# Sparse attention with a bilinear feed-forward layer: the second chunk's products no longer kept in DRAM, and the queries of a chunk loaded in two transfers

## The chip, the cores and the metric

The kernel runs on one core of a Trainium2 chip. The metric is the device time of one execution in microseconds; lower is better. Engines are written as in the profile: PE is TensorE, DVE VectorE, ACT ScalarE, POOL GpSimd, SP the engine whose queue issues transfers.

## What is computed

Four sequences of 768 tokens with 8 heads of 64 pass block-sparse attention; its output, laid out as a matrix x of 3072 x 512, passes a bilinear layer with 1536 inner features.

```python
def _attn_ref(q, k, v, sampled_blocks):             # q, k, v: (4, 8, 768, 64)
    scores = scale * np.matmul(q, k.transpose(0, 1, 3, 2))
    # blocks of 32: neighbours, the first and last block, 3 sampled blocks per row of blocks
    ...
    scores = np.where(mask, scores, -1000000000.0)
    attn = np.exp(scores - np.max(scores, axis=-1, keepdims=True))
    attn = attn / (np.sum(attn, axis=-1, keepdims=True) + 1e-09)
    return np.matmul(attn, v)

def _moe_ref(x, w_a, w_b, w_out):                   # x: (3072, 512)
    a = x @ w_a                                     # w_a, w_b: (512, 1536)
    b = x @ w_b
    return a * b @ w_out                            # w_out: (1536, 512)

x = attn_out.transpose(0, 2, 1, 3).reshape(B * S, H * D)
```

## The kernel before

**Chunks and units.** The 3072 tokens are cut into 12 chunks of 256, three for each sequence, and a chunk into 8 units of 32 tokens (one block). The chunks come in the order 1, 0, 2 for the first sequence and 0, 1, 2 for the others; "second chunk" means the second in this order, `cc == 1`. A unit in the middle of a sequence attends 8 blocks: POOL copies their keys into `KG`, SP's queue gathers their values into `VG`. The first and the last unit of a sequence attend all 768 tokens, in quads of heads (`attend_quad`).

**Attention of a unit.** PE makes the scores `s` (lines 772 and 873), DVE their maxima (`low`, line 888 or 975), ACT the exponentials `sm` (898 or 990), ACT or DVE a high and DVE a low half-precision part `hl` (790, 793, 797); a transposing transfer on SP's queue turns `hl` into `pt` (920, 1015), and PE multiplies `pt` with the values (`av`, 816). ACT and DVE write x as a high and a low part into `xT` (1060, 1063), which has two buffers, one for each parity of the chunk. `x_ready[cc]` fires when all of a chunk's x is written.

**Queries.** `queries(cc)` loads 64 x 2048 numbers of f32 (64 partitions, head by head, 256 tokens each) in one transfer from ACT's queue (634), takes a bound of them (642), scales them into the high part of `QT` (647), makes the low part (649) and has both copied to partitions 64 to 127 by two transfers on SP's queue (673).

**Feed-forward of a chunk.** It goes in 12 slices f of 128 features. `first_products` makes both products of a slice in `ab` (24 matmuls, line 1098; two buffers). `inner` has ACT scale the first into `a` (1126) and DVE multiply it by the second (1129). `split` makes `gh`, a rounded copy, on ACT (1153) and the rest `gl` on DVE (1156), two buffers each. `second_products` multiplies them by the slice of `w_out` into `o` (6 matmuls, lines 1184 to 1186). `store` copies `o` (1199, 1200) and writes the rows out (1203). The weights are loaded and split into parts during the first chunks (lines 693 to 753); `w_ready[f]` fires per slice.

**Parking.** With `PARK`, the second chunk's products take another way: `inner` stores `a` to a DRAM tensor `parked_g` (1134) in place of the split, and `unpark`, started when `second_products` comes to that chunk, loads each slice back into a buffer of `a` (1147; the tile is named `u`) and splits it there. The first products of the second chunk are a flow of their own, ranked one behind that of all other chunks, and the third chunk's first products wait for the last split of the second (`split_done`).

**The order of the work.** The instructions' order is set when the kernel is built, by a planner (`Plan`). Each piece of work is a generator (a flow) with a rank; it asks for a `Way`: an engine, a cost in ns, a function that issues the instructions, and for transfers the time that the DMA engines are taken to move. The planner keeps its own clock of each engine and of the DMA engines and issues at each step the request that can begin first; at equal times the lower rank goes first. Attention's ranks are its unit numbers, those of `second_products` 8000, of `first_products` 9000. So a changed cost or a removed flow changes the order of other work, too. Within an engine the instructions run in the order in which they were issued.

## Time and profile before

| | |
|---|---|
| median of 3 runs | 906.45 us (903.02 to 914.17) |
| profiled execution | 901.24 us |
| its span, first to last instruction | 899.5 us |
| mean granted TensorE clock | 0.977 |
| busy: PE, weight loads, DVE, ACT, POOL | 770.2, 619.3, 580.0, 464.3, 176.9 us |
| transfers | 145.50 MB, 212221 packets |

The profile is of one execution. Times are counted from the first instruction. "Busy" is the time in which an engine had at least one instruction running; issuing transfers is not counted. A wait is the idle time of an engine before an instruction, put down to what ended last of all that the instruction needed. The chain is followed back from the last instruction, at each step to what released it or to the instruction before it on its engine. A granted clock of 1 is TensorE's full speed.

### The profile page before, as it was taken

What the parts mean: (1) busy time and instruction counts of PE and PEld (TensorE: products, weight loads), DVE (VectorE), ACT (ScalarE), POOL (GpSimd) and SP (SyncE); (2) the same over time, 40 slices, a digit from 0 to 9 for tenths busy, and PEclk for the clock granted to TensorE, in tenths of its full rate; (3) what the DMA queues carried; (4) which work ended last, traced back from release to release, by engine and by line L of the source; (5) the groups of instructions that cost most, each with busy time, mean ns of one, the idle gap of its engine ahead of it and who ended that gap; (6) DMA issues with size and microseconds to landing.
All of it is one profiled execution on the core that took longest, in us unless ns stands there. A gap on an engine that the chain in (4) does not pass through costs nothing.

```text
span 899.5 us, 23840 instructions
## 1 busy us (share of the span) xinstructions
PE 770.2 (86%) x9024; PEld 619.3 (69%) x9024; DVE 580.0 (64%) x1533; ACT 464.3 (52%) x1118; POOL 176.9 (20%) x416
## 2 busy tenths in 40 slices
PE   0132499678989999999999899999998999999998
PEld 0022277557768777777777678788776878888886
DVE  3898999986558677665677577645867736342222
ACT  4675576586446566754456468335536424232222
POOL 0652142322003332110132331001322200000000
PEclk9998599899999999999999999999999999999999
DMA  9978999979878699985867999637766516351000
GB/s 228 287 186 218 243 235 252 222 193 206 215 205 181 140 194 210 198 181 136 173 155 170 180 211 206 153 82 159 180 134 155 125 29 153 80 121 27 25 1 24
DMA packets 212221, 145.50 MB, mean 162 GB/s; under 512 B 152841, under 2 KB 180490, under 8 KB 211338
## 3 DMA queue, kind: packets, MB, share of 16 engines
q1 hardware_dynamic: 201280, 106.22, 54.3%
q10 hardware_dynamic: 10826, 37.76, 14.4%
q8 instruction: 71, 1.16, 0.5%
q14 instruction: 44, 0.36, 0.1%
HBM read 87.82 MB, written 14.16 MB: 113 GB/s over the span
## 4 chain that ended last, share of the span: by engine, by line
PE 55%; DMA 14%; DVE 10%; ACT 7%; issue 2%; SPq 2%; ACTq 0%; POOL 0%
PE ab L1098 30%; PE o L1184 6%; PE av L816 5%; DMA pt<-hl 5%; PE o L1186 5%; PE o L1185 5%; DMA q<-in_q_dram 3%; PE s L772 3%; DVE low L888 1%; DVE hl L797 1%; DVE xT L1063 1%; DMA VG<-vd 1%; DVE QT L649 1%; DMA u<-parked_g 1%; ACT sm L898 1%
## 5 line engine op out<-in xcount | busy, mean ns | idle before, releaser
L1098 PE MATMUL ab<-xT,wab 128*128 128x256 f16 x3456 | 404.7, 274 | 12.7 <-ACT xT L1060 6.9
L1098 PEld LDWEIGHTS <-wab 128*128 128x128 f16 x3456 | 329.7, 98 | 78.5 <-issue 37.7
L1129 DVE SCALAR_TENSOR_TENSOR a<-a,rscale,ab 128x256 f32<-128x256 f32 x144 | 68.6, 478 | 112.1 <-ACT a L1126 110.9
L1184 PE MATMUL o<-woh,gh 128*128 128x512 f32 x288 | 127.1, 441 | 6.8 <-ACT gh L1153 6.4
L1126 ACT ACTIVATE a<-ab,f 128x256 f32<-128x256 f32 x144 | 67.5, 468 | 120.3 <-PE ab L1098 114.4
L898 ACT ACTIVATE sm<-s,low,cq 128x256 f32<-128x256 f32 x176 | 97.9, 559 | 58.7 <-DVE low L891 29.4
L816 PE MATMUL av<-pt,VG 128*128 128x64 f16 x2688 | 103.2, 196 | 28.9 <-DMA pt<-hl 14.9
L816 PEld LDWEIGHTS <-VG 128*128 128x128 f16 x2688 | 94.6, 100 | 48.1 <-issue 35.5
L573 POOL COPY KG<-keysT 128x384 int32<-128x384 int32 x88 | 56.9, 647 | 356.5 <-PE s L772 325.9
L797 DVE SCALAR_TENSOR_TENSOR hl<-sm,den,hl 128x256 f16<-128x256 f32 (+1 forms) x208 | 104.3, 510 | 21.4 <-ACT hl L790 18.6
L1186 PE MATMUL o<-woh,gl 128*128 128x512 f32 x288 | 115.2, 400 | 0.5 <-DVE gl L1156 0.5
L1185 PE MATMUL o<-wol,gh 128*128 128x512 f32 x288 | 113.6, 395 | 0.0
L578 POOL COPY KG<-keysT 128x128 int32 x264 | 94.5, 394 | 42.9 <-POOL KG L573 23.2
L1153 ACT CAST gh<-a 128x256 fp32r<-128x256 f32 x132 | 53.1, 403 | 59.2 <-DVE a L1129 58.0
L1156 DVE TENSOR_TENSOR gl<-a,gh 128x256 fp32r<-128x256 f32 x132 | 58.2, 441 | 32.3 <-ACT gh L1153 31.6
L1184 PEld LDWEIGHTS o<-woh,gh 128*128 128x128 f32 x288 | 54.7, 190 | 27.7 <-ACT gh L1153 10.0
L772 PE MATMUL s<-KG,QT 128*32 128x256 f16 x1408 | 58.8, 291 | 16.8 <-DMA QT<-QT 16.6
L873 PE MATMUL s<-mrows,ident 128*32 128x192 bf16 (+1 forms) x352 | 25.6, 280 | 54.7 <-ACT sm L898 27.8
L1063 DVE SCALAR_TENSOR_TENSOR xT<-av,xT 64x256 f16<-64x256 f32 x96 | 40.4, 421 | 44.3 <-ACT xT L1060 43.4
L1186 PEld LDWEIGHTS o<-woh,gl 128*128 128x128 f32 x288 | 54.6, 189 | 16.6 <-DVE gl L1156 4.3
L888 DVE TENSOR_REDUCE low<-s 128x2 f32<-128x512 f32 x88 | 59.9, 682 | 6.4 <-PE s L772 6.1
L772 PEld LDWEIGHTS <-QT 128*32 128x32 f16 x1664 | 43.7, 101 | 29.5 <-issue 24.1
(92 smaller groups left out, 736.0 us busy)
## 6 DMA issues: line engine op xcount, KB each, us to landing
VG<-vd SPq DMA_DIRECT2D x284, 64.0 KB, 2.2
VG<-vd SPq DMA_DIRECT2D x88, 192.0 KB, 3.3
VG<-vd SPq DMA_DIRECT2D x32, 384.0 KB, 3.8
q<-in_q_dram ACTq DMA_DIRECT2D x12, 512.0 KB, 6.0
QT<-QT SPq DMA_DIRECT2D x24, 256.0 KB, 3.8
vd<-vs SPq DMA_DIRECT2D x16, 384.0 KB, 4.1
out_dram<-ou SPq DMA_DIRECT2D x24, 256.0 KB, 2.4
stage<-in_k_dram ACTq DMA_DIRECT2D x12, 384.0 KB, 4.2
```

Of the source, the lines that this page charges most:

```text
L578: nc.gpsimd.tensor_copy(to[:, :, (5 + r) * w : (6 + r) * w], of[:, :, bass.ds(at, w)])
L772: mm(to[h * BLK : (h + 1) * BLK], q_block(cc, i, 4 * hq + h, a), rhs(4 * hq + h), start=(first and a == 0), stop=(a == 1), skip_group_chec ...
L797: t = yield dve(221 + n * 1.03, lambda: nc.vector.scalar_tensor_tensor(lo, sm, over, hi, ALU.mult, ALU.subtract))
L816: mm(av[:, g, i % 2, :], w, pt[:, y, cols], start=(i % 2 == 0 and g == 0 and first and n + m == 0), stop=(last and n == len(terms) - 1 and ...
L888: yield dve(685, lambda: nc.vector.tensor_reduce(mx, ps, axis=mybir.AxisListType.X, op=ALU.max, negate=True))
L898: t = yield act(750, lambda hq=hq: nc.scalar.activation(sm[:, hq], ps[:, hq], AF.Exp, bias=low[:, at, hq, 0:1], scale=cq[:, cc, hq : hq + ...
L1098: mm(ab[:, i, :], wab[:, f, i, part, kt, :], xc[:, kt, a, :], start=(i == 0 and kt == 0 and part + a == 0), stop=(kt == KT - 1 and a == 1) ...
L1126: yield act(470, lambda: nc.scalar.activation(a_sb, ab[:, 0, :], AF.Copy, scale=fb[:, f : f + 1]))
L1129: t = yield dve(420, lambda: nc.vector.scalar_tensor_tensor(a_sb, a_sb, rb, ab[:, 1, :], ALU.mult, ALU.mult))
L1184: mm(po, gh[:, js], woh[:, f, :], start=(f == 0), stop=False)
L1185: mm(po, gh[:, js], wol[:, f, :], start=False, stop=False)
L1186: mm(po, gl[:, js], woh[:, f, :], start=False, stop=(f == NF - 1))
```

## The change

The second chunk's slices go through `split` like those of all other chunks; `parked_g`, `unpark` and their events are gone; all chunks are one flow of `first_products`. The load of a chunk's queries is cut by heads into two transfers of 4 heads each, whose contiguous run is 4 x 256 x 4 = 4096 bytes instead of 8192. The planner's cost for it is 950 ns of the issuing queue instead of 475; the 1400 ns of moving stay.

```diff
--- before.py
+++ after.py
@@ -53,7 +53,6 @@
 LEAD_K, LEAD_V, LEAD_Q, LEAD_X, LEAD_G = 10, 9, 8, -1, 2
 GATE_KV, GATE_Q, GATE_G = 10, 5, 4
 R_W, R_W_STEP = 8, 0.2
-PARK = True
 W_PE, W_DVE, W_ACT, W_POOL, W_SP = 0, 1, 0, 0, 2
 SLACK = 0
 R_NOW, R_P2, R_P1 = -50, 8000, 9000
@@ -631,7 +630,12 @@
         yield from gate(u0 - GATE_Q)
         freed = yield from take("rq", 1)
         t = work.tile([P, H, CH], F32, tag="rq", name=f"q{cc}", bufs=1)
-        yield load_way(1400, lambda: nc.scalar.dma_start(t[:D], q[b, c]))
+
+        def load():
+            for hs in (slice(0, H // 2), slice(H // 2, H)):
+                nc.scalar.dma_start(t[:D, hs], q[b, c][:, hs])
+
+        yield [Way("LOAD", 950, load, 1400, 1)]
         if cc + 1 < NC:
             b1, c1 = chunks[cc + 1]
             plan.start(queries(cc + 1), order[b1, c1 * PER] - LEAD_Q)
@@ -1069,24 +1073,19 @@
             read.fire(left.at + LATE_AV)
 
 
-    parked_g = dram.tile([NF, P, CH], F32, name="parked_g")
-    g_parked = [Event() for _ in range(NF)]
-    split_done = [Event() for _ in range(NF)]
     ready = {(cc, f): Event() for cc in range(NC) for f in range(NF)}
     parts = {}
     f1_ready = {(b, f): Event() for b in range(B) for f in range(NF)}
 
-    def first_products(ccs):
-        for cc in ccs:
+    def first_products():
+        for cc in range(NC):
             b, c = chunks[cc]
             xc = xT[cc % 2]
             yield x_ready[cc]
-            if cc == 2 and PARK:
-                yield split_done[NF - 1]
             if cc == 0:
                 plan.start(second_products(), R_P2)
             for f in range(NF):
-                if cc < 2 and (cc == 0 or PARK):
+                if cc == 0:
                     yield w_ready[f]
                 read = yield from take("ab", 2)
                 ab = psum.tile([P, 2, CH], F32, tag="ab", name=f"ab{cc}_{f}", bufs=2)
@@ -1130,22 +1129,7 @@
             a_sb, a_sb, rb, ab[:, 1, :], ALU.mult, ALU.mult
         ))
         read.fire(t)
-        if cc == 1 and PARK:
-            t = yield sp(650, 364, lambda: nc.sync.dma_start(parked_g[f], a_sb))
-            e_a.fire(t)
-            g_parked[f].fire(t)
-            return
         yield from split(cc, f, a_sb, e_a)
-
-    def unpark():
-        for f in range(NF):
-            yield g_parked[f]
-            if f >= 2:
-                yield split_done[f - 2]
-            e_a = yield from take("a", A_BUFS)
-            a_sb = work.tile([P, CH], F32, tag="a", name=f"u{f}", bufs=A_BUFS)
-            t = yield sp(650, 364, lambda f=f: nc.sync.dma_start(a_sb, parked_g[f]))
-            plan.start(split(1, f, a_sb, e_a), R_NOW, t)
 
     def split(cc, f, a_sb, e_a):
         e_h = yield from take("gh", 2)
@@ -1157,15 +1141,11 @@
         e_a.fire(t)
         parts[cc, f] = (gh, gl, e_h, e_l)
         ready[cc, f].fire(t + LATE_G)
-        if cc == 1 and PARK:
-            split_done[f].fire(t)
 
     def second_products():
         banks, o_read = [None] * NJ, [None] * NJ
         for cc in range(NC):
             b, c = chunks[cc]
-            if cc == 1 and PARK:
-                plan.start(unpark(), R_NOW)
             rows = out[b * S + c * CH : b * S + (c + 1) * CH, :].rearrange(
                 "(j p) d -> j p d", j=NJ
             )
@@ -1216,11 +1196,7 @@
         plan.start(gather_keys(0), -LEAD_G)
         plan.start(gather_values(0), -LEAD_G)
         plan.start(attend(*units[0]), 0)
-        if PARK:
-            plan.start(first_products([0, *range(2, NC)]), R_P1)
-            plan.start(first_products([1]), R_P1 + 1)
-        else:
-            plan.start(first_products(range(NC)), R_P1)
+        plan.start(first_products(), R_P1)
         plan.run()
```

## Rows read from the trace of the kernel before

**Rows 1.** The stages: busy time of each engine in four stretches of the execution (stretch and its length in us; busy us and number of instructions of TensorE, its weight loads, VectorE, ScalarE, GpSimd; granted TensorE clock as a share of full speed; busy share of the DMA engines; GB/s).

```profile
0.00:112.00 112.00, 26.14 (x425) 18.65 (x426) 87.00 (x209) 65.12 (x141) 36.91 (x69) 0.89 0.89 233
112.00:192.40 80.40, 68.40 (x798) 54.45 (x797) 75.29 (x198) 54.26 (x131) 25.80 (x46) 0.92 0.95 232
192.40:268.70 76.30, 66.94 (x747) 52.47 (x747) 48.39 (x126) 42.77 (x100) 8.46 (x23) 0.98 0.85 203
268.70:810.00 541.30, 523.08 (x6389) 423.36 (x6389) 348.08 (x956) 281.80 (x702) 105.78 (x280) 1.00 0.70 154
```

**Rows 2.** The chain that ended last, its shares by engine (from the page).

```profile
PE 55%; DMA 14%; DVE 10%; ACT 7%; issue 2%; SPq 2%; ACTq 0%; POOL 0%
```

**Rows 3.** The same table of stretches for line 1098 alone, the matmuls of the first products (TensorE, weight loads, then clock, DMA share, GB/s).

```profile
112.00:192.40 80.40, 37.27 (x288) 29.03 (x287) 0.92 0.95 232
192.40:268.70 76.30, 33.31 (x288) 27.56 (x289) 0.98 0.85 203
```

**Rows 4.** The timeline of VectorE: the last write of the second chunk's x (start us, us, instruction, and in brackets the idle time before it and what ended it).

```profile
191.11 0.43 DVE L1063 SCALAR_TENSOR_TENSOR xT<-av,xT 64x256 f16<-64x256 f32 x1 [0.23 <-ACT xT L1060]
```

**Rows 5.** The transfers between 192 and 268.7 us: all packets, and the two issues of the parking (count, KB each, median us to landing).

```profile
DMA packets 27375, 15.51 MB, mean 202 GB/s; under 512 B 17538, under 2 KB 25442, under 8 KB 27366
...
parked_g<-a SPq DMA_DIRECT2D x12, 128.0 KB, 2.0
u<-parked_g SPq DMA_DIRECT2D x12, 128.0 KB, 3.1
```

**Rows 6.** The instructions of lines 1134 and 1147, the store and the load of the parked products, on SP's queue (duration ns min/median/max, first and last start us).

```profile
L1134 SPq DMA_DIRECT2D parked_g<-a x12: 320/382/560, 202.2 to 254.9; - x12
...
L1147 SPq DMA_DIRECT2D u<-parked_g x12: 362/540/912, 209.0 to 258.6; - x12
```

**Rows 7.** The waits of ScalarE between 192 and 270 us (us in all, times, longest).

```profile
ACT gh L1153 <- DMA u<-parked_g: 16.8, 9, 3.4
```

**Rows 8.** Pieces of the chain that ended last, between 196 and 275 us (start us, us, what).

```profile
211.74 5.91 DMA parked_g<-a
...
249.41 2.32 DMA u<-parked_g
...
252.36 3.19 DMA u<-parked_g
...
258.55 3.26 DMA u<-parked_g
```

**Rows 9.** The timeline of TensorE: the start of the first chunk's first products, and places between 215 and 270 us (start us, us, instruction, idle time before it and what ended it).

```profile
111.97 0.59 PE L1098 MATMUL ab<-xT,wab 128*128 128x256 f16 x2 [6.03 <-ACT xT L1060]
112.86 3.75 PE L1098 MATMUL ab<-xT,wab 128*128 128x256 f16 x22 [0.30 <-DVE xT L1063]
...
215.05 0.88 PE L816 MATMUL av<-pt,VG 128*128 128x64 f16 x24 [1.95 <-DMA pt<-hl]
...
218.77 2.78 PE L1098 MATMUL ab<-xT,wab 128*128 128x256 f16 x24 [0.44 <-DVE a L1129]
...
256.09 0.50 PE L1184 MATMUL o<-woh,gh 128*128 128x512 f32 x1
...
257.59 0.70 PE L816 MATMUL av<-pt,VG 128*128 128x64 f16 x18
...
262.35 0.79 PE L1184 MATMUL o<-woh,gh 128*128 128x512 f32 x1 [2.39 <-ACT gh L1153]
...
265.08 0.90 PE L816 MATMUL av<-pt,VG 128*128 128x64 f16 x18
...
268.75 0.38 PE L1098 MATMUL ab<-xT,wab 128*128 128x256 f16 x2 [0.85 <-ACT xT L1060]
269.65 2.56 PE L1098 MATMUL ab<-xT,wab 128*128 128x256 f16 x22 [0.52 <-DVE xT L1063]
```

**Rows 10.** Waits between 268.7 and 810 us, of TensorE and of ScalarE (us in all, times, longest).

```profile
PE o L1184 <- ACT gh L1153: 4.1, 6, 1.4
...
ACT QT L642 <- DMA q<-in_q_dram: 12.7, 7, 3.7
```

**Rows 11.** The twelve loads of the queries, line 634 (duration of the issue in ns min/median/max, first and last start; then the time to landing).

```profile
L634 ACTq DMA_DIRECT2D q<-in_q_dram x12: 472/483/529, 8.5 to 669.0; - x12
...
DMA to landing us min/median/max: 4.9/6.0/8.9
```

**Rows 12.** The shortest and the longest of the five loads of queries among the long pieces of the chain after 300 us (start us, us, what).

```profile
482.17 4.79 DMA q<-in_q_dram
...
669.03 7.34 DMA q<-in_q_dram
```

**Rows 13.** Packets, MB and share of the 16 engines' time of one DMA queue (q10 carries ScalarE's transfers, q1 SP's), in three stretches: 483.4 to 486 us, one load of queries (64 of the 80 packets are data); 31.3 to 43.5 us, weights; 463.7 to 466.4 us, two copies inside QT (128 of the 154 are data).

```profile
q10 hardware_dynamic: 80, 0.52, 82.3%
...
q10 hardware_dynamic: 863, 3.14, 76.4%
...
q1 hardware_dynamic: 154, 0.53, 91.8%
```

**Rows 14.** The table of stretches again, for three short ones (columns as in rows 1).

```profile
112.80:116.60 3.80, 3.73 (x28) 2.90 (x28) 3.60 (x14) 3.61 (x11) 0.32 (x1) 0.67 0.86 213
228.00:252.00 24.00, 24.00 (x234) 19.20 (x232) 12.60 (x30) 8.60 (x22) 0.00 (x0) 1.00 0.82 210
262.30:265.10 2.80, 2.75 (x7) 1.85 (x8) 1.58 (x5) 2.71 (x7) 0.00 (x0) 0.50 0.95 209
```

## The prediction, made before the change was run

> **What bounds the kernel now.** I read the stages first, then the chain of waits, then the waits of each engine in the stage that the change touches, then the transfers. The stages [rows 1] show a kernel of two kinds. Up to 192.4 us TensorE is idle for almost 98 us (26.14 busy of 112, then 68.40 of 80.4), while VectorE is busy for 75.29 of 80.4 us and the DMA engines for 0.95 of the stretch: weights, keys and tables set the pace. From 268.7 to 810 us TensorE is busy for 523.08 of 541.3 us, and the chain of waits [rows 2] is mostly TensorE (55%). From there on the end is the sum of TensorE's work, and a few microseconds saved earlier arrive at the end if no new idle time appears. The reader is to see that between these lies one stretch, 192.4 to 268.7 us, with 9.4 us of idle time (76.3 less 66.94), and that the parked products live there.
>
> That the parking never lets a product run early is the first thing to see. TensorE has exactly 288 matmuls of the first products before 192.4 us and 288 after it, up to 268.7 [rows 3]: 12 slices of 24 each, the first chunk and then the second. The second chunk's begin there because its last piece of x is written from 191.11 for 0.43 us, not because weights are late [rows 4]. So without parking the flow can start at the same moment, in the same order. What parking does is to put a store and a load between a product and its split, and to hold chunk 1's second products back: the first slice is stored at 202.2 and the last loaded from 258.6 [rows 6].
>
> **The change part by part: no parking.** Removed are 24 issues on SP, 12 of 382 ns and 12 of 540 ns at the median [rows 6], 11.1 us of that queue together, and 24 x 128 KB = 3.1 MB of the 15.51 MB that the transfers move in this stretch [rows 5]. Nothing of the arithmetic goes: a, gh, gl and both products stay, 24 + 6 matmuls a slice. ScalarE's copy gh waited for reloaded products 9 times, 16.8 us in all [rows 7]. Since ScalarE runs in order, what is queued behind those waits is the attention's exponentials. On the chain of waits four pieces are parking: 5.91, 2.32, 3.19 and 3.26 us, 14.7 us [rows 8]. But their whole length is not the price, as TensorE worked beside most of it.
>
> The price is read from TensorE. (a) At 262.35 it had waited 2.39 us for gh, the last reloaded slice, queued in front of the attention's av at 265.08 [rows 9]. [...] (c) At 218.77 it waited 0.44 us for an a whose buffer a store still held (the piece of 5.91 us in [rows 8]) [rows 9]. (d) At 268.75 and 269.65 it waited 0.85 and 0.52 us for the last x of the third chunk [rows 9]. That x follows the av which stood behind (a) in TensorE's order. Together 2.39 + 1.23 + 0.44 + 1.37 = 5.43 us. What is late next is the attention of the last unit of the third chunk, through its transposes (pt<-hl ended a wait of 1.95 us on TensorE at 215.05 [rows 9]).
>
> The bounds: at best all 9.4 us of idle time and the 1.2 us of slow clock go, 10.6 us. At worst nothing goes: up to 268.7 us the same work waits for the same x, and idle time only moves to behind the last second product, which then comes earlier. That could even cost: after 6.03 us of idle time at 111.97 the 22 matmuls of a slice took 3.75 us, against 2.56 for as many at 269.65 [rows 9], so 1.2 us (the granted clock was 0.67 there [rows 14]), and some 2 with the matmuls around it. I take 5.4, since it is made of waits whose releaser is named; the range keeps -10.6 to +2.
>
> The new coupling: a slice of chunk 1 now needs one of the two gh and gl buffers, which the second products free. The second products rank before the first, and such a pair of slice and second product is what the kernel does in every later chunk, where gh is waited for 4.1 us in 541 [rows 10]. I cost it at nothing; cover gone, that is a tenth of those 4.1 us for one chunk of ten, 0.4 us. The removed wait of the third chunk for the last split is worth nothing: that split was done before its second product ended at 265.08, and x came at 269.65 [rows 9].
>
> **Queries in two transfers.** Twelve loads become twenty-four. Each has one more issue on ScalarE's queue, 483 ns at the median [rows 11], 5.8 us over the kernel, hidden as ScalarE is busy for 281.80 of the long stage's 541.30 us [rows 1]; without that cover, 0.5 us before the exponentials at each chunk. The load takes 6.0 us at the median to land [rows 11], and ScalarE waits for it 12.7 us in seven places of the long stage [rows 10]. Five are among the long pieces of the chain there, 4.79 to 7.34 us each [rows 12]. What can halving the run do? A load moves 64 partitions of 8192 bytes: 82.3% of 16 engines for 2.6 us over 64 data packets, 535 ns each [rows 13]. Two prices for 4096-byte packets are in the trace. Weights, 128 partitions: 76.4% of 16 engines for 12.2 us over 3.14 MB = 767 packets, 194 ns each. Copies inside QT, 64 partitions: 91.8% for 2.7 us over 128 packets, 310 ns [rows 13]. At the weights' price a load would be (64 x 535 - 128 x 194)/16 = 0.59 us shorter; at QT's, (128 x 310 - 64 x 535)/16 = 0.34 us longer, and its second half is issued 0.48 us later. The load has 64 partitions like QT, so I take QT's side and, as the transfer's length is only part of the 6.0 us, a cost of zero, with both ends kept: five pieces on the chain at -0.6 to +0.8 us are -3 to +4 us.
>
> [...]
>
> **The sum.** The profiled execution took 901.24 us, its span 899.5. Less 5.4 that is 895.8. It stands 5.2 us below the median of the three runs, 906.45, which spread over 11 us. The prediction is of a median, so 906.45 - 5.4 = 901. Planning is done anew for the whole program, and other orders may fall out by ties; that has no row and only widens the range.
>
> **Rivals.** All of them are given from the median.
> (1) The idle time only moves. For it: the third chunk's x comes from the attention, whose transposes also end TensorE's waits in this stretch, and DMA is busy for 0.85 of it. Against it: av stands behind the reloaded slice in TensorE's own order. Time 906.45 + 0 to 2: 907.
> (2) All of it goes, and the queries follow the weights' price: -10.6 - 3: 893. For it: 16.8 us of ScalarE's waits and 11.1 us of SP's queue go, much more than 9.4. Against: TensorE was busy for 24 of 24 us between 228 and 252 [rows 14], so that waits of other engines cost it nothing there.
> (3) Slower: the second half of the queries lands late. It is issued last and shares the 16 engines with the transposes and gathers of SP's queue, and the landing already varies from 4.9 to 8.9 us [rows 11]. If every load on the chain came at the late end, 2.9 us past the median, five pieces would be 14.5 us, less 5.4 saved: 915. It decides from 5.4/5 = 1.1 us of lateness per load. For it: ScalarE runs in order and waits for q already. Against it: in the long stage TensorE has other work at hand, and its whole idle time there is 18 us.
>
> **How the numbers follow.** Forecast 0.50, rival 1 0.22, rival 2 0.14, rival 3 0.14. The likeliest one's own range is 895 to 908: the terms of 2 to 8 us, and half of the spread of runs. The range reaches toward 893 less a few microseconds of spread and to rival 3 at 915: 888 to 914. Faster by over 2% means under 888.3, slower by over 2% above 924.6; 2% is about what a measurement of this kernel can tell from no change. Only the far tail of rival 2 with a lucky new order passes the first, 0.08, and rival 3 with more than five loads the second, 0.07; 0.85 is left.
>
> **What would show it.** Right: no parked_g rows, gh of chunk 1 waits for a and not for a transfer; the second products of chunk 1 begin near 205, before the first reload was issued at 209.0 [rows 6], and end by about 256; the third chunk's first slice starts 4 to 7 us before 268.75; busy time of TensorE within 3 us of 770; queries' packets of about 300 ns, landing of the second half 5.5 to 7 us. Wrong: the third chunk's first slice at 267 or later (rival 1), idle time of TensorE beyond 268.7 us over 25 us with waits for QT (rival 3), or a first slice of the first chunk moved by more than 3 us from 112, which would mean that the new plan of the start, not this stage, decides.

## The result, and the profile after

The changed kernel took 910.85 us at the median of 22 runs (904.97 to 921.02), the kernel before 905.85 us at the median of 22 beside them. The ratio is 1.0071, interval [1.0046, 1.0096]: slower by 0.7%, where 0.6% faster was forecast. Run again (label e10_change_again) it was at 1.0028 [0.9984, 1.0072], which alone does not exclude no change. So by the two it is slower by some 0.3 to 0.7%, 3 to 6 us. Both of its profiled executions lie in the slow part of its runs (921.02 us, the slowest of the 22, and 913.55 us beside a median of 909.69; the rows below are from the second), so that what only these two show is not taken for a cause, and e1 and e8 further down, which share its order or nearly so, stand beside them.

The stages of the changed kernel, cut at the first slice of the first, second, third, fourth, fifth and eighth chunk (columns as in [rows 1]):

```profile
110.00:193.20 83.20, 71.86 (x798) 55.89 (x798) 75.91 (x200) 54.49 (x133) 24.32 (x46) 0.88 0.92 225
193.20:264.80 71.60, 66.00 (x780) 52.79 (x780) 48.40 (x129) 42.49 (x102) 10.88 (x28) 0.98 0.77 170
264.80:341.70 76.90, 69.63 (x896) 55.23 (x892) 50.27 (x141) 39.01 (x98) 22.34 (x59) 0.96 0.78 154
341.70:411.40 69.70, 64.00 (x716) 52.00 (x713) 46.47 (x127) 42.83 (x100) 13.92 (x33) 0.95 0.85 188
411.40:614.30 202.90, 194.17 (x2343) 154.92 (x2340) 130.87 (x362) 108.21 (x265) 38.61 (x100) 0.99 0.72 160
614.30:907.80 293.50, 288.65 (x3092) 236.34 (x3088) 141.11 (x373) 111.70 (x280) 30.24 (x82) 1.00 0.39 93
```

The kernel before, cut in the same way behind the stretches that stand in [rows 1]:

```profile
268.80:338.20 69.40, 67.23 (x923) 53.59 (x922) 51.46 (x149) 42.66 (x109) 23.80 (x62) 1.00 0.82 172
338.20:401.00 62.80, 60.66 (x692) 48.70 (x688) 43.10 (x115) 40.56 (x96) 13.96 (x36) 1.00 0.91 197
401.00:601.60 200.60, 192.16 (x2362) 154.86 (x2362) 131.72 (x366) 106.97 (x264) 37.25 (x100) 1.00 0.75 164
601.60:895.80 294.20, 288.62 (x3091) 236.49 (x3086) 142.21 (x374) 111.91 (x280) 30.68 (x82) 1.00 0.40 93
```

Length less TensorE's busy time is its idle time. In the second chunk's stretch, which the forecast was about, that fell from 9.4 us [rows 1] to 5.6, and the DMA share from 0.85 to 0.77. Behind the third chunk's first slice it rose: 2.2 to 7.3, 2.1 to 5.7, 8.4 to 8.7, 5.6 to 4.9; in all 18.3 to 26.5 us. And the granted clock of the third and the fourth chunk is 0.96 and 0.95 of full speed where it was 1.00: in the third, 896 matmuls are busy for 69.6 us where 923 were for 67.2.

The first products alone (TensorE, weight loads, clock, DMA share, GB/s), which answer to [rows 3], and the places that answer to [rows 9]:

```profile
110.00:193.20 83.20, 39.78 (x288) 30.22 (x288) 0.88 0.92 225
193.20:264.80 71.60, 33.20 (x289) 27.53 (x290) 0.98 0.77 170
```

```profile
109.96 0.58 PE L1097 MATMUL ab<-xT,wab 128*128 128x256 f16 x2 [6.24 <-ACT xT L1064]
...
264.75 0.38 PE L1097 MATMUL ab<-xT,wab 128*128 128x256 f16 x2
265.40 2.56 PE L1097 MATMUL ab<-xT,wab 128*128 128x256 f16 x22 [0.27 <-DVE xT L1067]
...
278.01 0.35 PE L877 MATMUL s<-mrows,ident 128*32 128x192 bf16 x4 [3.18 <-ACT sm L902]
...
335.23 0.62 PE L776 MATMUL s<-KG,QT 128*32 128x256 f16 x16 [2.15 <-DMA QT<-QT]
...
346.52 2.78 PE L1097 MATMUL ab<-xT,wab 128*128 128x256 f16 x24 [1.37 <-DVE a L1128]
...
354.67 0.66 PE L1164 MATMUL o<-woh,gh 128*128 128x512 f32 x1 [1.79 <-ACT ou L1179]
...
378.89 4.36 PE L1097 MATMUL ab<-xT,wab 128*128 128x256 f16 x24 [2.53 <-DVE a L1128]
```

The wait of 0.85 us at the third chunk's x is gone, and that of 2.39 us for a reloaded slice, too; the slice stands 4.0 us before 268.75, but 2.0 of these are the first chunk's, which began that much earlier. In the first profiled execution it stands at 270.45, later than before, as the stretch from the first to the second chunk's first slice took 86.6 us there (80.4 before, 83.2 here). The stretch from the second to the third, which the change touches, is the same in both, 71.4 and 71.6 us, and was 76.3. After the third chunk's first slice come five idle times of 1.4 to 3.2 us with four different releasers, in a stretch where the kernel before waits for gh (2.1 us in three), sm (1.2) and x (1.4), and for little else. The last row shows slow work behind such a wait: 24 matmuls took 4.36 us there, behind 2.53 us of idle time, and 2.78 at 346.52, behind 1.37. In the first profiled execution the same two took 4.40 us behind 2.49, at a granted clock of 0.61 (383.5 to 387.9 us), and 2.78 behind 1.25, at 1.00 (351.2 to 354.0).

### The profile page after: what moved, and what is told of

Read it like the earlier page. It is cut to its first block, busy times and chain, and to the rows that moved or that the text cites. A ratio compares the mean times of both kernels' runs of the same rounds, so it can differ in the third digit from the quotient of the medians.

```text
span 919.2 us, 23808 instructions
## 1 busy us (share of the span) xinstructions
PE 783.6 (85%) x9024; PEld 628.0 (68%) x9024; DVE 581.4 (63%) x1537; ACT 464.1 (50%) x1114; POOL 177.1 (19%) x416
## 3 DMA queue, kind: packets, MB, share of 16 engines
q10 hardware_dynamic: 11786, 37.76, 15.3%
## 4 chain that ended last, share of the span: by engine, by line
PE 50%; DMA 14%; DVE 13%; ACT 6%; issue 4%; SPq 2%; ACTq 0%; POOL 0%; POOLq 0%; DVEq 0%
PE ab L1097 27%; DMA pt<-hl 6%; PE o L1164 5%; PE av L820 5%; PE o L1166 5%; PE o L1165 5%; DMA q<-in_q_dram 5%; PE s L776 3%; DVE QT L653 2%; DVE hl L801 2%; DVE a L1128 1%; DVE xT L1067 1%; DMA VG<-vd 1%; ACT xT L1064 1%; DMA QT<-QT 1%
## 5 line engine op out<-in xcount | busy, mean ns | idle before, releaser
L1097 PE MATMUL ab<-xT,wab 128*128 128x256 f16 x3456 | 410.7, 277 | 14.1 <-DVE a L1128 6.4
L572 POOL COPY KG<-keysT 128x384 int32<-128x384 int32 x88 | 60.4, 687 | 356.3 <-PE s L776 335.2
L1166 PE MATMUL o<-woh,gl 128*128 128x512 f32 x288 | 117.4, 408 | 1.8 <-DVE gl L1140 1.4
L1165 PE MATMUL o<-wol,gh 128*128 128x512 f32 x288 | 115.5, 401 | 0.0
L577 POOL COPY KG<-keysT 128x128 int32 x264 | 91.7, 384 | 36.5 <-POOL KG L572 24.2
L1137 ACT CAST gh<-a 128x256 fp32r<-128x256 f32 x144 | 58.1, 403 | 68.4 <-DVE a L1128 65.6
L1140 DVE TENSOR_TENSOR gl<-a,gh 128x256 fp32r<-128x256 f32 x144 | 64.0, 445 | 27.9 <-ACT gh L1137 27.4
L776 PE MATMUL s<-KG,QT 128*32 128x256 f16 x1408 | 59.9, 295 | 20.2 <-DMA QT<-QT 20.1
L1164 PEld LDWEIGHTS o<-woh,gh 128*128 128x128 f32 x288 | 55.6, 193 | 25.9 <-issue 9.6
L797 DVE TENSOR_SCALAR hl<-sm,den 128x256 f16<-128x256 f32 (+1 forms) x123 | 44.2, 363 | 39.6 <-DMA pt<-hl 39.6
```

Of the source, the lines that this page charges most:

```text
L577: nc.gpsimd.tensor_copy(to[:, :, (5 + r) * w : (6 + r) * w], of[:, :, bass.ds(at, w)])
L776: mm(to[h * BLK : (h + 1) * BLK], q_block(cc, i, 4 * hq + h, a), rhs(4 * hq + h), start=(first and a == 0), stop=(a == 1), skip_group_chec ...
L1097: mm(ab[:, i, :], wab[:, f, i, part, kt, :], xc[:, kt, a, :], start=(i == 0 and kt == 0 and part + a == 0), stop=(kt == KT - 1 and a == 1) ...
L1140: t = yield dve(430, lambda: nc.vector.tensor_sub(gl, a_sb, gh.bitcast(F32)))
L1164: mm(po, gh[:, js], woh[:, f, :], start=(f == 0), stop=False)
L1165: mm(po, gh[:, js], wol[:, f, :], start=False, stop=False)
```

## The experiments

Several orders of the same work are compared, so the terms of all the profiled executions stand in one table. "Start" is where the first chunk's first slice begins; "idle 1" is TensorE's idle time from there to the third chunk's first slice, "idle 2" from there to the end, "busy" its busy time after the start. Start, idle 1, idle 2 and busy add up to the last matmul's end, 5.4 to 5.8 us before the execution's time. Single executions of one kernel differ by about 1% (the row of e5 is 7.3 us below the median of its runs, that of before 3 to 5 below, that of e10 3.9 above), so a row shows where time lies, and the ratio says how much.

| kernel | order | start | idle 1 | idle 2 | busy | execution | ratio to before |
|---|---|---|---|---|---|---|---|
| before | old | 112.0 | 21.4 | 18.3 | 744.1 | 901.24 | |
| e3_two_transfers_old_plan | old | 113.3 | 20.1 | 15.6 | 750.7 | 905.36 | 0.9965 [0.9932, 0.9999] |
| e2_two_transfers | near old | 116.1 | 22.2 | 14.9 | 746.2 | 905.19 | 0.9974 [0.9942, 1.0007] |
| e4_one_transfer_new_plan | near old | 112.0 | 18.9 | 16.4 | 748.0 | 900.81 | 1.0019 [0.9977, 1.006] |
| e5_kept_on_chip_old_order | old | 115.0 | 15.7 | 11.9 | 742.4 | 890.51 | 0.9954 [0.9916, 0.9992] |
| e14_kept_on_chip_old_order_again | old | 116.9 | 17.8 | 15.3 | 747.7 | 903.14 | 0.9967 [0.9925, 1.0009] |
| e7_kept_on_chip_two_transfers | old | 114.1 | 15.5 | 14.4 | 745.7 | 895.37 | 0.9977 [0.9943, 1.0011] |
| the change, first | new | 112.5 | 19.6 | 25.9 | 757.4 | 921.02 | 1.0071 [1.0046, 1.0096] |
| e10_change_again | new | 110.0 | 16.9 | 26.5 | 754.4 | 913.55 | 1.0028 [0.9984, 1.0072] |
| e1_no_parking | new | 116.1 | 12.6 | 24.5 | 746.3 | 904.95 | 1.0024 [0.998, 1.0068] |
| e8_kept_on_chip_uncounted | near new | 113.9 | 13.3 | 25.7 | 750.6 | 908.94 | 1.0028 [0.9988, 1.0068] |
| e9_no_parking_counted | third | 115.7 | 18.2 | 22.4 | 747.1 | 908.74 | 1.0023 [0.9984, 1.0062] |
| e6_no_parking_keys_early | fourth | 112.1 | 13.4 | 23.3 | 747.1 | 901.44 | 0.9954 [0.9914, 0.9994] |
| e6_no_parking_queries_early | fifth | 107.9 | 13.5 | 26.4 | 748.2 | 901.36 | 0.9934 [0.9896, 0.9972] |
| e12_no_parking_queries_early_again | fifth | 109.2 | 15.9 | 24.1 | 747.8 | 902.52 | 0.9927 [0.9887, 0.9967] |
| e13_change_queries_early | fifth | 106.0 | 15.6 | 30.4 | 749.3 | 907.06 | 0.998 [0.9943, 1.0017] |

"Old" is the order of the kernel before on every engine, the transfers apart that were taken out or cut in two. The order of the changed kernel differs from it in 1,354 of TensorE's 17,186 instructions, that of e8 in 1,394 (the expectations count both sides of a difference, so 2,788). A plan made anew also moves a few pieces of work between ScalarE and VectorE, where either can do them. Without parking but with one transfer (e1) it is the same as the changed kernel's on every engine, the issues of the queries apart.

### Which half of the change: parking or the two transfers

The first four kernels take one half each. Theory P: taking out the parking costs the time; theory Q: the queries' second transfer does. No parking, queries in one transfer:

```diff
-PARK = True
+PARK = False
```

> The kernel before with the parking alone taken out; the queries still come in one transfer of 8192-byte runs. Theory P (taking out the parking is what costs: chunk 1's slices now wait for gh and gl, and the order planned anew leaves idle time on TensorE after the third chunk begins): ratio to before 1.005 to 1.009, +4 to +8 us, with the third chunk's first slice no earlier than 267 us and more than 25 us of TensorE idle time behind it. Theory Q (the queries' second transfer is what costs, and the parking's removal saves what was forecast): ratio 0.993 to 0.997, -3 to -6 us, third chunk's first slice at 262 to 265 us.

Measured: 909.01 us, ratio 1.0024, between the ranges of the two theories. The third chunk's first slice comes 148.6 us after the start (264.7 less 116.1), in the kernel before 156.8: the saving is there and larger than forecast. Behind it the idle time is 24.5 us.

Parking kept, queries in two transfers, with the planner's new cost, with its old cost, and the new cost with one transfer:

```diff
-        yield load_way(1400, lambda: nc.scalar.dma_start(t[:D], q[b, c]))
+        def load():
+            for hs in (slice(0, H // 2), slice(H // 2, H)):
+                nc.scalar.dma_start(t[:D, hs], q[b, c][:, hs])
+        yield [Way("LOAD", 950, load, 1400, 1)]     # e2; e4: one dma_start
+        yield load_way(1400, load)                  # e3
```

> The kernel before, with parking, and only the queries' load changed: two transfers of 4096-byte runs, planned at 950 ns. Theory P: ratio 0.998 to 1.002. Theory Q: 1.008 to 1.014, +8 to +12 us, because the saving of the parking is not there to set against it; landing of the second half later than 6.5 us at the median.

> The kernel before, with parking, the queries' load in two transfers but planned at the old cost of 475 ns: every engine's order is that of the kernel before, except that each of the 12 issues on ScalarE's queue is two. This is the transfers' own price with no new order. Theory P: ratio 0.998 to 1.002. Theory Q: as the run with the new cost, 1.008 to 1.014. If this one is at 1.000 and the other is above 1.004, the price lies in the order that the new cost makes.

> The kernel before, with parking, the queries in one transfer as before, but planned at the new cost of 950 ns, so that only the order planned anew is in it (460 of 17186 rows of TensorE's order move, 63 of 1469 of VectorE's). Theory P and theory Q: 0.998 to 1.002. A third theory, that any new order of the start moves this kernel by half a per cent: 1.003 or more to either side.

Measured: 0.9974, 0.9965 and 1.0019 of before. With parking, in the old order and in the one next to it (e2 and e4 differ by the cut alone), two transfers cost nothing and may give a third to half of a per cent. The half that was forecast to save is the one that does not, and the half that was costed at nothing is not the culprit, with parking at least.

### The round trip or the order

Theory O: the round trip through DRAM is worth about what the prediction said, and the order planned anew gives it back. Theory S: it is the structure, any third chunk that begins earlier runs into the loads behind it. If O holds, the saving must show when it is taken out and nothing else moves. In e5 the twelve slices stay on the chip: eight in a buffer that the queries do not need then, the others in the buffers of a. The 24 transfers are not issued, but the planner still counts them, and so every engine's order stays the old one.

```diff
+        if cc == 1 and 3 <= f < 11:
+            a_sb = kept_g["box"][:, f - 3]
...
-            t = yield sp(650, 364, lambda: nc.sync.dma_start(parked_g[f], a_sb))
+            t = yield sp(650, 364, lambda: None)
...
-            t = yield sp(650, 364, lambda f=f: nc.sync.dma_start(a_sb, parked_g[f]))
+            a_sb = kept_g[f]
+            t = yield sp(650, 364, lambda: None)
```

> The kernel before, but the second chunk's slices wait in on-chip memory (8 of them in the queries' buffer, idle at that time, 4 in the buffers of a) instead of DRAM: the 24 transfers are gone, the planner still counts them, and every engine's order is that of the kernel before. So this takes out the round trip alone. Theory O (taking out the round trip is worth what was forecast, and what gave it back in the kernel without parking is the order planned anew): ratio 0.992 to 0.996, -4 to -7 us; TensorE idle 3 to 5 us between the second and the third chunk's first slice (9.4 before), and 16 to 19 us behind it (18.3 before). Theory S (any earlier start of the third chunk runs into loads of keys and queries that cannot come earlier, whatever the order): idle time behind it 22 to 26 us as without parking, ratio 0.999 to 1.003.

Measured: 897.78 us, 0.9954 [0.9916, 0.9992]; again on another chip (e14) 0.9967 [0.9925, 1.0009]. That is 3 to 4 us, not far from the 5.4 forecast. The idle times were not where theory O had them: 6.1 us between the second and the third chunk's first slice (3 to 5 expected), and 11.9 behind the third's (16 to 19 expected).

> The slices kept on the chip in the old order, again: 0.992 to 0.999 of before, with the third chunk's first slice at least 5 us nearer to the first chunk's than in before, where 156.8 us lay between them, and 11 to 15 us of idle behind it. Over 1.000 would undo the case that the round trip's removal is worth the forecast.

In that second run the slice came only 1.1 us nearer to the start (155.7 after 156.8), a miss against the 5 expected: its idle time up to there is 3.6 us less than before, but TensorE is busy for 2.6 us more (the granted clock of the two stretches is 0.89 and 0.95, before 0.92 and 0.98). The idle time behind the third chunk, 15.3 us, is just over the bound.

Then the same kernel with the planner free: e8 leaves the 24 empty entries out (`yield sp(650, 364, lambda: None)` goes, twice, and with it the time that it returned), and nothing else. Theory S now stands for what e5 leaves of it: that the separate flow of the second chunk's slices, which e5 and e8 have and the changed kernel has not, is what is worth having.

> The kernel before with its parked slices kept on the chip, as in the experiment that kept the old order, but the planner no longer counts the 24 transfers of 364 ns, so that the order of the work is its own choice again: it comes out within 924 rows of TensorE's of the order of the kernel without parking, and 2,788 rows from the order of before. Theory O (the order planned anew gives the saving back): ratio to before 0.999 to 1.005, near the 1.0024 of the kernel without parking, with 22 to 26 us of TensorE idle behind the first slice of the third chunk where the same structure in the old order had 11.9. Theory S (the separate flow of the second chunk's slices is what is worth having): ratio 0.994 to 0.998 as in the old order, idle behind the third chunk 12 to 16 us.

Measured: 908.07 us, 1.0028 [0.9988, 1.0068]. The two kernels do the same arithmetic on the same buffers with the same transfers. The stretches of the third and fourth chunk and the waits of TensorE in them, first in the old order (e5), then as planned anew (e8):

```profile
265.20:332.70 67.50, 66.72 (x923) 53.80 (x923) 50.79 (x148) 43.09 (x109) 24.08 (x60) 1.00 0.84 179
332.70:395.40 62.70, 60.55 (x692) 48.67 (x688) 43.03 (x115) 40.42 (x96) 14.30 (x36) 1.00 0.95 197
```

```profile
PE s L873 <- ACT sm L898: 1.6, 2, 1.3
PE ab L1098 <- ACT xT L1060: 0.9, 1, 0.9
PE o L1191 <- ACT gh L1160: 0.6, 2, 0.4
```

```profile
263.40:335.80 72.40, 68.60 (x890) 55.25 (x890) 50.10 (x144) 37.53 (x94) 22.25 (x59) 0.98 0.78 160
335.80:404.10 68.30, 62.73 (x719) 51.47 (x716) 45.97 (x125) 43.40 (x102) 13.82 (x33) 0.98 0.87 192
```

```profile
PE s L873 <- ACT sm L898: 2.8, 3, 2.4
PE o L1189 <- ACT ou L1204: 2.1, 1, 2.1
PE ab L1098 <- DVE a L1136: 1.8, 1, 1.8
PE av L816 <- DMA pt<-hl: 1.3, 1, 1.3
PE s L772 <- DMA QT<-QT: 1.2, 1, 1.2
```

The reader is to see the changed kernel's waits again in e8, for sm, ou, a and QT, at the same places, though e8 has the queries in one transfer and the second chunk in a flow of its own. What these two and e1 share is the order, or nearly. With the order held the removal gives 3 to 4 us in two runs; planned anew, the same instructions cost some 2.5 us (nothing, by the low end of the interval). So on time e8 speaks for theory O and against the separate flow. The first form of theory S does not explain e5, whose third chunk began as early after the start as e8's (150.2 and 149.5 us) and met no such waits.

Is it that the plan was looser where it counted the transfers? e9 is the kernel without parking, with two empty entries for each of the second chunk's slices:

```diff
+        if cc == 1:
+            yield sp(650, 364, lambda: None)
+            yield sp(650, 364, lambda: None)
         yield from split(cc, f, a_sb, e_a)
```

> The kernel without parking, one flow for all chunks, but the planner counts two transfers of 364 ns on the queue of SP for each slice of the second chunk, which are not issued. Its order is then 1,412 rows of TensorE's from the old order and 2,784 from that of the kernel without parking. Theory O: ratio 0.993 to 0.999, idle behind the third chunk's first slice 12 to 18 us, with the waits for query copies, key loads and sums of the third chunk's stretch gone or under 1 us. Theory S: ratio 1.000 to 1.006, and idle behind the third chunk 22 us or more, as in the kernel without parking.

Measured: 1.0023, idle 2 of 22.4 us, both where theory S had them: a miss for O. S has fallen with e8, where the separate flow did not help; what e9 takes away from O is that counting the transfers makes a good order. Its order is a third one, as little good as the new one. So there is no slack to put back: the old order fell out well at this place, and the new one and e9's fell out worse.

### Two transfers on the chip's own terms

e7 is e5 with the queries in two transfers at the old cost.

> The kernel with the slices kept on chip in the old order, and the queries' load in two transfers at the old planned cost: both parts of the change without any new order. Theory O: the two prices add, -5 us and -3 us: ratio 0.988 to 0.993, faster than both kernels. Theory S: 0.996 to 1.000.

> The changed kernel again, on the same chip as the next. Against it only the queries' load differs: two issues of 4096-byte runs here, one there, in one order otherwise. If the split's price is one for all orders, the two are 0.3% apart with this one the faster (as the two kernels with the old order were); if it depends on what the queries' loads meet, this one is 0.3 to 0.7% the slower, near 1.007 of before, with more ScalarE wait for q.

> The kernel without parking and with the queries in one transfer, again, beside the changed kernel: 1.000 to 1.005 of before, 23 to 26 us of TensorE idle behind the third chunk's first slice, and that slice 3 to 6 us earlier than before where the first chunk begins at the same time.

e7 stood at 0.9977: a miss for O, the two prices do not add. e10 stood at 1.0028 and e11 at 1.0039 [1.0, 1.0077] (909.69 and 910.17 us), which is neither of the two differences expected of e10; e11 has no row in the table, as its profiled execution took 1168.67 us at a granted clock of 0.68. With e13 below there are five pairs on one chip each, alike but for the cut: two transfers less one is -0.35% (e3 and before), -0.45% (e2 and e4), +0.23% (e7 and e5), -0.11% (e10 and e11), +0.53% (e13 and e12). Each ratio has an interval of about 0.4% to either side, and no sign holds. The prediction's -3 to +4 us (-0.3 to +0.4%) is about as far as it can be told.

### Other orders

Two settings of the planner let the loads go earlier: the keys' by two units, the queries' by one. Both are tried without parking (the line `PARK = False` is left out here), the second also with the whole change.

```diff
-GATE_KV, GATE_Q, GATE_G = 10, 5, 4
+GATE_KV, GATE_Q, GATE_G = 10, 6, 4   # queries early
+GATE_KV, GATE_Q, GATE_G = 12, 5, 4   # keys early
```

> No parking, queries in one transfer, and the queries' load allowed one unit earlier (gate 6 units ahead instead of 5), planned anew. In the run without parking TensorE waited 2.1 us for QT at 332.9 us. Theory O: that wait goes, and with another order the idle time behind the third chunk's start comes to 15 to 22 us (24.5 without this edit): ratio 0.994 to 1.001. Theory S: 23 to 27 us, ratio 1.001 to 1.006.

> No parking, queries in one transfer, and the keys' and values' loads allowed two units earlier (gate 12 units ahead instead of 10), planned anew. In the run without parking ScalarE waited 5.0 us for keys at 332.3 us, and TensorE then 1.3 and 1.8 us at 343.1 and 351.2. Theory O: these waits shrink and the idle time behind the third chunk's start comes to 18 to 22 us: ratio 0.996 to 1.001. Theory S: 23 to 27 us, ratio 1.001 to 1.006.

> The kernel without parking with the queries' load let go one unit earlier, again on another chip. Theory O as it stands (idle behind the third chunk's first slice is what decides): with its 26 us there it should stand at 0.998 to 1.004, and the 0.9934 measured before came from runs whose first chunk began early. If 0.990 to 0.997 comes again, the start of this order is truly earlier, by about 4 us at the first chunk's first slice (107.9 against 112.0), and the theory must hold the stretch before the first chunk as well.

> The whole change with the queries' load let go one unit earlier: the order of the kernel before it in this list but for the issues of the queries. Theory O: within 0.5% of that kernel, whatever its ratio, and at least 0.3% faster than the changed kernel's 1.003 to 1.007. If the two transfers cost something where the queries meet other loads: 0.5% or more above it.

Without parking they stood at 0.9934 and 0.9954, and the first again at 0.9927 [0.9887, 0.9967] on another chip: the lowest ratio of the study, 899.48 us beside 904.27. But the reason given for it failed. Idle 2 is 24 to 30 us with the queries early, and 23.3 with the keys early. What is better with the queries early is the start, 106.0 to 109.2 us in its three profiles, against 110.0 to 116.9 in all the others. So the theory of the order must hold the stretch ahead of the first chunk as well as that behind the third; with idle 2 alone it does not give these ratios. For the keys' order, with a start of 112.1, neither gives its 0.9954, and that stays open. The whole change in the order with the queries early stood at 0.998 [0.9943, 1.0017], not slower than before, so the change is not bound to lose. It is 0.53% above e12, where its expectation put the border between no cost and a cost of the two transfers; the intervals do not tell which.

## Why the prediction was wrong, step by step

**The stretch with the parking: right, in kind and about in size.** Steps (a), (c) and (d) name 4.2 us of idle time. The 1.23 us that the sum adds to them, the slow clock of the bounds, are the 2.73 us of the six matmuls from 262.35 less the 1.50 of those from 256.09 [rows 9]; from 262.3 to 265.1 the granted clock was 0.50, and 1.00 from 228 to 252 [rows 14]. At that place of the changed kernel six such matmuls took 1.48 us (from 258.85 to the next start). But the stretch as a whole stayed at a granted clock of 0.98 in both executions, as before [rows 1], and in the first execution six such matmuls took 2.72 us from 224.65, at 0.50 (224.6 to 227.4), soon after 2.89 us of idle time that ended at 223.13. In this stretch the idle time fell from 9.4 us to 5.6 and 5.5 in the two executions of the changed kernel, to 3.2 in e1, and to 6.1 and 6.3 in e5 and e14; the stretch itself became 4.8 and 4.9 us shorter in the changed kernel. No wait for a reloaded slice is left. The forecast that the third chunk's first slice starts 4 to 7 us earlier came true by 4.0 us in one execution, half of it by an earlier start, and failed in the other (270.45), where the stretch ahead was longer. That only idle time moves (rival 1) is not what e5 shows. The second products began later than "near 205", at 208.0, and ended at 270.2, not at 256: the new order puts 780 matmuls between the two first slices where there were 747 [rows 1], and leaves some of the second chunk's products for later.

**The new coupling at nothing: not contradicted.** gh is not among TensorE's waits in the second chunk's stretch of the changed kernel, and not in those of the third and the fourth.

**Queries in two transfers at zero: not contradicted, and not told closer than half a per cent.** The row below answers to [rows 13]: the two transfers of one chunk's queries, 551 to 555 us (packets, MB, share of the 16 engines' time).

```profile
q10 hardware_dynamic: 160, 0.52, 53.1%
```

These 0.531 x 16 x 4.0 = 34.0 us are for 128 packets of 4096 bytes, one chunk's queries; the 64 of 8192 bytes were 34.2 (82.3% of 16 engines for 2.6 us). That is 265 ns a packet (34.0/128), between the weights' 194 and QT's 310, and the same in all: the shorter run gave nothing to this load of 64 partitions. What sets these prices, no run here shows. ScalarE's wait for the queries in the kernel before, and then the time to landing (of each half, from its own issue) and the wait in the changed one:

```profile
ACT QT L642 <- DMA q<-in_q_dram: 19.2, 9, 5.0
```

```profile
DMA to landing us min/median/max: 3.9/5.6/9.7
...
ACT QT L646 <- DMA q<-in_q_dram: 19.9, 8, 5.4
```

4.9/6.0/8.9 us [rows 11] became 3.9/5.6/9.7, and 19.2 us of waits 19.9. But these are two orders. In the new order alone ScalarE's waits for the queries are 14.9 us with one transfer (e1), and 19.9 and 23.6 with two (the changed kernel's two executions); in the old order 19.2 and 16.0 (before and e3). One place in the new order, in e1 and then in e10:

```profile
370.05 1.91 ACT L642 ACTIVATE QT<-q 64x2048 f16<-64x2048 f32 x1 [2.22 <-DMA q<-in_q_dram]
...
373.12 2.78 PE L1098 MATMUL ab<-xT,wab 128*128 128x256 f16 x24 [1.76 <-DVE a L1129]
```

```profile
375.82 1.91 ACT L646 ACTIVATE QT<-q 64x2048 f16<-64x2048 f32 x1 [3.10 <-DMA q<-in_q_dram]
...
378.89 4.36 PE L1097 MATMUL ab<-xT,wab 128*128 128x256 f16 x24 [2.53 <-DVE a L1128]
```

ScalarE waits 0.9 us longer for the queries there, TensorE 0.8 us longer for a, and its 24 matmuls take 1.6 us more; the first execution has the same (2.49 and 4.40 us). So a little of rival 3, the late second half, is in the traces of this order; its 14.5 us are not, and e10 and e11 do not differ in time. That the second transfer costs time there is not shown. Rival 3's sign in the profile, idle time of over 25 us with a wait for QT, did come and would have misled: e1 has the same wait for QT (2.1 us) and 24.5 us of idle time with one transfer. A sign that two causes can give tells nothing until one of them is taken out.

**The step that failed.** "A few microseconds saved earlier arrive at the end if no new idle time appears", with "other orders may fall out by ties; that has no row and only widens the range". The new plan of the whole program was a term of the sum, put at nothing without a row, and it is as large as the saving: with the order held the removal stands at 0.9954 and 0.9967 of before, planned anew at 1.0028 (e8), which is 0.6 to 0.7%, 5 to 7 us, more. A part of it is seen as idle 2: seven profiles of the old order or one near it have 11.9 to 18.3 us, nine of orders planned anew without the transfers 22.4 to 30.4. It is not the whole price of an order, as the fourth and the fifth have 23.3 to 30.4 us of it and are not slower than before. For the changed kernel, against the execution before: start -2.0, idle 1 -4.5, idle 2 +8.2, busy +10.3, in all +12.0 of 12.3 us, over twice what the medians give; for e1, whose clock fell less (0.98 and 1.00 in the third and the fourth chunk, 0.96 and 0.95 in the changed kernel), +4.1, -8.8, +6.2, +2.2. TensorE's whole busy time, forecast within 3 us of 770, was 780.6. Of the 10.3 us more, 7.8 lie behind the third chunk's first slice, with the granted clock of the third and fourth chunk at 0.96 and 0.95 (before 1.00); 3.5 lie ahead of the second chunk's (0.88, before 0.92), where e1 has 2.9 more, and 1.0 less between the two.

**What the order does at one place.** ScalarE in the changed kernel (start us, us, instruction, idle time before it):

```profile
331.08 0.33 ACTq L471 DMA_DIRECT2D stage<-in_k_dram  x1
...
334.11 0.19 ACT L481 ACTIVATION_READ_ACCUMULATOR ks<-stage 128x1 f32 x1
340.74 0.84 ACT L481 ACTIVATE ks<-stage 128x768 f16<-128x768 f32 x1 [6.45 <-DMA stage<-in_k_dram]
...
345.50 0.46 ACT L1125 ACTIVATE a<-ab,f 128x256 f32<-128x256 f32 x1
```

and in the kernel before:

```profile
326.28 0.33 ACTq L472 DMA_DIRECT2D stage<-in_k_dram  x1
...
333.65 0.51 ACT L790 ACTIVATE hl<-sm,den 128x256 f16<-128x256 f32 x1 [4.78 <-DMA pt<-hl]
...
335.31 0.83 ACT L482 ACTIVATE ks<-stage 128x768 f16<-128x768 f32 x1
```

In the new order the second load of keys is issued at 331.08, and its reader stands 3.2 us behind the issue in ScalarE's queue (334.30, when the instruction before it ends). The plan allows 1241 + 1000 + 1200 ns = 3.4 us for such a load when the DMA engines are free; here it took until 340.74, 9.7 us. All that ScalarE does waits behind it, the copy of the product (345.50) with it, though that product was complete at 340.06 (24 matmuls from 337.27, 2.79 us) and ScalarE stood idle for another 1.61 us ahead of 343.29, waiting for an instruction in front of the copy; and TensorE waits 1.37 us for a at 346.52. From 343.29 on ScalarE works off what has piled up, with one idle time of 0.31 us, up to the copy `ou` at 354.03, for which TensorE waits 1.79 us at 354.67. e1 and e8 have the same wait for keys (4.98 and 4.93 us) and for `ou` (1.80 and 2.15). In the old order the same reader came 9.0 us behind its issue, and found the keys there. But ScalarE stood idle in the kernel before, too, 4.78 us for a transpose, and TensorE waited behind it, once:

```profile
335.05 0.50 PE L1184 MATMUL o<-woh,gh 128*128 128x512 f32 x1 [1.39 <-ACT gh L1153]
```

So an idle ScalarE is no price by itself: the place cost TensorE 1.39 us in the old order and 3.16 in the new one, 1.8 us of the 8.2 by which idle 2 grew.

Not settled: how the rest of the new order's price comes about, which of the instructions that changed places would bring the old idle time back, and why the first slice of the first chunk is earlier with the queries early. No single move was tried. The sums of e10 and before are from one execution each.

## What to carry to other kernels

Where the order of the instructions is planned at build time from costs, removing work changes two things, the work and the plan; price them apart, by removing the work with the order held (leave its entries in the plan, empty) and then letting the plan go. A saving of half a per cent is smaller than what another order of the same work does here (0.993 to 1.004 of before, without parking), so it is worth trying some settings of the planner with each change. And before a saving ahead of a busy stretch is counted as time at the end, look at the readers of loads in that stretch: one that stood as near behind its issue as the plan allows waited here (3.2 us behind a load of 9.7), and one that stood 9.0 us behind did not. That is one place, and no test of its own.

## What the runs showed of the hardware

A load of 384 KB of keys took 3.1 us to land at the least, 4.7 at the median and 10.0 at the most in the changed kernel (e10), and 2.8 to 7.3 in the one before. For the reader that stood 3.2 us behind its issue it was the load of 9.7 us that counted, not the median.

A slice of 24 matmuls of one form took 2.78 us and 4.36 us within 33 us of each other in e10, after 1.37 and 2.53 us of idle time. In the first execution of the changed kernel the two took 2.78 and 4.40 us, after 1.25 and 2.49 us, at a granted clock of 1.00 and 0.61. In e1 the second of them took 2.78 us after 1.76 us of idle time, in a stretch (338.3 to 404.1 us) at 1.00. Behind the third chunk's first slice, 6 to 8 us more of idle time than in the kernel before came with 1.6 (e1), 5.7 (e8), 7.8 (e10) and 10.3 us (the first execution of the changed kernel) more of busy time. So the busy time that came with more idle time varied between executions by more than the change was worth.
